# Chunked attention, low-rank mixer and channel MLP on one core: loads planned with their time on the DMA engines, and the first pair's x and low-rank part summed in PSUM

## The chip, the core and the metric

The kernel runs on one core of a Trainium2 chip. The metric is device time in microseconds (us); three runs of the kernel before gave a median of 1002.67. The profile is one execution on the same core, read by engine: PE (TensorE; its weight loads are PEld), DVE (VectorE), ACT (ScalarE), POOL (GpSimd) and SP (SyncE). SP and POOL matter here because they issue the transfers from HBM, each on a queue of its own.

## The reference

Eight batches, eight heads, 576 positions of 64 values. Attention stays within chunks of 64 positions. Its output, put together as x of 576 x 512 per batch, goes through a mixer of rank 32 over the positions, and then through an MLP over the channels (512 to 2048 and back):

```python
q_c, k_c, v_c = (a.reshape(B, H, S // 64, 64, D) for a in (q, k, v))
scores = np.matmul(q_c, k_c.transpose(0, 1, 2, 4, 3)) / np.sqrt(D)
scores = scores - np.max(scores, axis=-1, keepdims=True)
attn = np.exp(scores)
attn = attn / (np.sum(attn, axis=-1, keepdims=True) + 1e-09)
x = np.matmul(attn, v_c)                       # -> (8, 576, 512)
...
h = x.transpose(0, 2, 1) @ U @ V               # U 576x32, V 32x576
u = x + h.transpose(0, 2, 1)
out = u + np.maximum(u @ w_ch1, 0.0) @ w_ch2   # 512 -> 2048 -> 512
```

U, V and both channel weights are float64; q, k and v are float32.

## The kernel before

**Tiling.** Batches are taken in four pairs. A pair has 2 x 576 = 1152 rows, nine tiles of 128 rows (T0 to T8; tile 4 holds rows of both batches, so it has two *segments*, the others one). Three tiles form a group of 384 rows (g = 0, 1, 2). The hidden dimension is cut into 16 blocks f of 128; W0 to W15 are the pieces of both weights that belong to a block.

**A tile's way through attention.** SP loads q and k (L388, L389), POOL loads v in pair 0 (L399). PE transposes q and k (L419, written `ps_qT`, `ps_kT`), ACT copies them out, PE multiplies for the scores (`sc`, L441), DVE takes the maximum and subtracts it (L455, L459), ACT takes the exponential (L463), PE transposes that (`ps_eT`), and multiplies by v (`av`, L472); DVE divides by the sum and gives x (L490).

**Mixer.** PE forms y = transposed U times x, in plain f32 in pair 0 (L559, five products of 512 columns per batch), and ACT and DVE round it to `ys` (L574, L575). Then, for each tile, four steps: `low_rank` (L592) multiplies V by ys into a PSUM bank `u`, one product of 512 columns for each segment; `add` (L598) adds it to x on DVE; `transposed` (L604) transposes the sum on PE in four blocks of 128 x 128 into a bank `ut`; and ACT and DVE split that into a high part `uth` (L612) and a low part `utl` (L617).

**MLP.** For a group and a block f, `hidden` multiplies 12 times into a bank h (L638, 384 columns), ACT and DVE turn this into `hh` and `hl` (L646, L651), and `project_out` adds three products of 512 columns for each tile into its bank `o` (L664), which collects all 16 blocks. At the end `finish` (L676) adds x and SP stores the result. Since `add` wrote into x, this x is u.

**Weights.** The float64 words are made into f32 on the chip: one ACT pass, six DVE steps (L92 to L101) and then a rounded high part and a low part (ACT L348, DVE L351) for each piece. DVE does this beside all that is told above.

**What sets the order.** In pairs 1 to 3 the attention and mixer steps are strewn by rule between the products of the MLP. Pair 0, with all weight pieces, is ordered by a planner when the program is built. Each piece of work is an `Op` with an engine, an estimated time `us`, what it comes after, a delay `lat` before other engines may use it, and the buffers it takes and frees. `order()` gives, for one engine after another, the ready op that can start first or stands first by rank; ranks come from three lists: `LOADS` (transfers), `WORK` (T tile, P the y of a batch, M the mixing of a group, U, V, W) and `STRETCHES` (group, first and last block f of the MLP). The result is a fixed sequence on each engine, and each engine keeps it: a waiting instruction holds all behind it. Into PE's planned idle time before the first mixing the planner puts products of no use (`fill`, L138, bfloat16), 41 in all.

SP and POOL may have eight transfers each on the way; each new one waits for the one eight before it, and for its buffer.

Of the kernel before, what the change touches and what calls it, by code (L numbers as in the profile page):

```python
# [21 lines left out]
def kernel(  # L22
# [11 lines left out]
    nc = tc.nc  # L34
# [5 lines left out]
    P = 128  # L40
    C = 64
# [69 lines left out]
    rank = [0]  # L111

    class Op:
        def __init__(self, eng, us, run, *after, take="", free="", lat=0.1):
            self.eng, self.us, self.run, self.lat = eng, us, run, lat
            self.after = [o for o in after if o is not None]
            self.take, self.free = take.split(), free.split()
            self.rank = rank[0], len(ops)
            ops.append(self)
# [25 lines left out]
    def order():  # L145
        free_at = {}
        stock = {k: [0.0] * n for k, n in ROOM.items()}
        waits = {o: len(o.after) for o in ops}
        users = {o: [] for o in ops}
        for o in ops:  # L150
            for p in o.after:
                users[p].append(o)
        ready = {o: 0.0 for o in ops if not o.after}
        hot = None
        out = []
        while ready:
            best = {}
            for o, t in ready.items():
                t = max(t, free_at.get(o.eng, 0.0))
                need = {k: o.take.count(k) for k in o.take}  # L160
                if any(len(stock[k]) < n for k, n in need.items()):
                    continue
                for k, n in need.items():
                    t = max(t, sorted(stock[k])[n - 1])
                best.setdefault(o.eng, []).append((t, o))
            if not best:
                raise RuntimeError(f"the plan has no way on: {[(o.name, o.eng, o.rank, o.take) for o in ready]} {stock}")
            picks = []
            for c in best.values():
                t0 = min(t for t, _ in c) + 0.05  # L170
                picks.append(min(((t, o) for t, o in c if t <= t0), key=lambda z: z[1].rank))
            t, o = min(picks, key=lambda z: (z[0], z[1].rank))
            us = o.us
            if o.eng == "PE":
                if o.name == "hidden" and hot is None:
                    hot = t + 3.5
                us *= COLD if hot is None or t < hot else 1.0
            end = t + us
            del ready[o]
            free_at[o.eng] = end  # L180
            for k in o.take:
                stock[k].remove(min(stock[k]))
            for k in o.free:
                stock[k].append(end)
            o.start, o.end = t, end
            for u in users[o]:
                waits[u] -= 1
                if not waits[u]:
                    ready[u] = max(p.end + (p.lat if p.eng != u.eng or p.lat > 1 else 0.0) for p in u.after)
            out.append(o)  # L190
        assert len(out) == len(ops), "some of the plan is left"
        return out
# [34 lines left out]
    def u_ops():  # L227
        st = {}

        def load():  # L230
            words = wslot((10, 2 * R), U32, "uraw")
            nc.vector.memset(words[:, 4:6], 0)
            nc.gpsimd.dma_start(words[:, 0:4], moe_U[0 : 4 * P].rearrange("(t p) r -> p t r", p=P))
            nc.gpsimd.dma_start(words[0:C, 4], moe_U[4 * P : S])
            nc.gpsimd.dma_start(words[C:P, 5], moe_U[0:C])
            nc.gpsimd.dma_start(words[:, 6:10], moe_U[C:S].rearrange("(t p) r -> p t r", p=P))
            st["raw"] = words.rearrange("p t (r w) -> p t r w", w=2)

        def room():
            st["u"] = wslot((10, R), U32, "uroom")  # L240
            return st["u"]

        def whole():

            st["f"] = u32 = wslot((10, 4, R), F32, "ust32")
            v = st["u"].bitcast(F32)
            nc.gpsimd.memset(u32[:, :, 3, :], 0.0)
            for j in range(3):
                nc.scalar.copy(u32[:, :, j, :], v)
            ust32.append(u32)  # L250

        def high():
            for j in range(4):
                nc.scalar.copy(ust[:, :, j, :], st["u"].bitcast(F32))

        def low():
            nc.vector.tensor_sub(ust[:, :, 3, :], st["u"].bitcast(F32), ust[:, :, 3, :])

        ld = Op("POOL", 2.7, load, take="w", lat=2.0)
        o, _ = rounding(Later(lambda: st["raw"]), room, ld, "w", 10 * R)  # L260
        w = Op("ACT", 1.4, whole, o, take="w", free="w")
        h = Op("ACT", 1.8, high, w)
        lo = Op("DVE", 0.5, low, h, free="w")
        h.rank = lo.rank = 0.5, len(ops)
        return w
# [5 lines left out]
    def v_ops():  # L271
        nc.vector.memset(vst[:, 0:C].bitcast(F32), 0.0)
        nc.vector.memset(vst[:, C + S :].bitcast(F32), 0.0)
        n = S // 4
        st = {}

        def load():
            words = wslot((2 * n,), U32, "vraw")
            nc.gpsimd.dma_start(words, moe_V.rearrange("r (b c) -> (r b) c", b=4))
            st["raw"] = words.rearrange("p (r w) -> p r w", w=2)  # L280

        def room():
            st["v"] = wslot((n,), U32, "vroom")
            return st["v"]

        def join():
            st["rows"] = dram.tile([R, S], F32, name="vrows")
            nc.gpsimd.dma_start(st["rows"].rearrange("r (b c) -> (r b) c", b=4), st["v"].bitcast(F32))

        def spread():  # L290
            st["all"] = wslot((S,), F32, "vall")
            for j in range(4):
                nc.gpsimd.dma_start(st["all"][j * R : (j + 1) * R], st["rows"])

        def high():
            nc.scalar.copy(vst[:, C : C + S], st["all"])

        def low():
            rows = slice(2 * R, 3 * R)
            dst = vst[rows, C : C + S]  # L300
            nc.vector.tensor_sub(dst, st["all"][rows], dst)

        ld = Op("POOL", 0.7, load, take="w", lat=2.5)
        o, _ = rounding(Later(lambda: st["raw"]), room, ld, "w", n)
        o = Op("POOL", 0.6, join, o, free="w w", lat=2.5)
        o = Op("POOL", 2.0, spread, o, take="w", lat=2.5)
        o = Op("ACT", 0.7, high, o)
        return [Op("DVE", 0.77, low, o, free="w")]

# [10 lines left out]
    def w_ops(f, after=None):  # L320
        st = {}
# [9 lines left out]

        n = 1 if f < NF - XROOM else 2
        size = 2 * DM // n
        ld = Op("SP", 3.2, load, after, take="w", lat=2.0)
        halves = []
        for z in range(n):
            cols = slice(z * size, (z + 1) * size)
# [73 lines left out]
    def attention_ops(pr, t, after=None):  # L411
# [75 lines left out]
        def scaled(e):  # L487
# [9 lines left out]

        src = lambda z: loaded[pr, t][z].rearrange("p h d -> p (h d)")
        flat = lambda: st["ex"].rearrange("p a b k -> p (a b k)")
        lq = Op("SP", 3.4, lambda: load_qk(pr, t), after, take="w" if mine else "slot slot slot", lat=1.6)  # L500
        tq = Op("PE", 0.55, lambda: transpose(src(0), "qT_"), lq, begun.get((pr, t - 2)), take="bank")
        lv = Op(
            "POOL" if mine else "SP",
            2.5,
            lambda: load_v(pr, t, q_last.get(ahead.get(t)) if mine else None),
            lq,
            lat=2.2,
        )
        if mine:
            tqs[t], lvs[t] = tq, lv  # L510
# [71 lines left out]
    def mix_ops(pr, t, x, ys, after=None, first=None):  # L582
# [31 lines left out]
        def low():  # L614
            uh, ul = ut_of[pr, g]
            js = slice(j * P, (j + 1) * P)
            nc.vector.tensor_sub(ul[:, :, js], st["t"].rearrange("p (c t) -> p c t", c=NCC), uh[:, :, js])  # L617

        segs = len(list(segments(pr, t)))
        lr = Op("PE", 0.23 * segs, low_rank, x, after, *(ys[b - 2 * pr] for _, _, b, _ in segments(pr, t)), *v_done, take="bank")  # L620
        ad = Op("DVE", 0.69, add, lr, free="bank")
# [34 lines left out]
    def project_out(pr, g, f, hs, first, final, j):  # L656
        hh, hl = hs
        t = g * GT + j
        if first:
            acc[g, j] = bank(f"o_{pr}_{t}")  # L660
        js = slice(j * P, (j + 1) * P)
        prods = [(hh, 0), (hh, 1), (hl, 0)]
        for i, (h, z) in enumerate(prods):
            nc.tensor.matmul(  # L664
                acc[g, j],
                lhsT=h[:, js],
                rhs=w2[f][:, z],
                start=(first and i == 0),
                stop=(final and i == 2),
            )  # L670
        return acc[g, j]
# [42 lines left out]

    LOADS = "W0 T1 T0 T3 T4 W1 T2 V T5 T8 U W2 T6 T7 W3 W4 W5 W6 W7 W8 W9 W10 W11 W12 W13 W14 W15".split()
    WORK = "U T3 T4 T8 T5 T2 T1 T7 T0 T6 W0 P0 P1 V M0 M1 W1 W2 W3 W4 W5 W6 W7 W8 W9 W10 W11 W12 W13 W14 W15".split()
    STRETCHES = ((0, 0, 2), (1, 0, 2), (0, 2, 3), (1, 2, 3), (0, 3, 4), (1, 3, 4), (0, 4, 5), (1, 4, 5), (0, 5, 6), (1, 5, 6), (0, 6, 7), (1, 6, 7), (0, 7, 8), (1, 7, 8), (0, 8, 9), (1, 8, 9), (0, 9, 10), (1, 9, 10), (0, 10, 11), (1, 10, 11), (0, 11, 12), (1, 11, 12), (0, 12, 13), (1, 12, 13), (0, 13, 14), (1, 13, 14), (0, 14, 16), (1, 14, 16))
    GATES = (28, 30)  # L720
    BASE = 1000
    u_done = None
# [170 lines left out]
```

## Time and profile before

| | us |
|---|---|
| median of three runs (lowest, highest) | 1002.67 (1002.03, 1004.46) |
| the profiled execution | 1002.66 |
| its span | 1000.9 |
| PE busy in the span | 980.2 (98%) |
| DVE busy | 405.6 (41%) |
| ACT busy | 256.9 (26%) |
| PE's products h and o, their three largest groups together | 1048.1 with overlap |

The groups of the page give busy time and mean duration of one instruction. PE's products overlap, so that a group's sum exceeds the time that it takes on the clock, and the distance from one start to the next is the better price. The mean granted TensorE clock of the execution was 0.994. A row of the timeline gives start, duration, engine, line and operation with its count, and in brackets the idle time ahead of it and what ended it.

### The profile page before, as it was taken

The numbers are of one execution on the slowest core, as the hardware profiler recorded it, in microseconds if no ns is written. First come the engines' busy times: TensorE is split into PE (matmuls) and PEld (weight loads), VectorE is DVE, ScalarE is ACT, GpSimd is POOL, SyncE is SP. The second block draws the span as 40 slices with busy tenths as digits, with TensorE's granted clock in tenths as the row PEclk, the third lists the DMA queues.
The fourth block names the chain that finished last, engine by engine and source line by source line (L and its number), as shares of the span: only waits on it lengthen the run. The fifth ranks groups of instructions, "written<-read, shape, count | busy, mean of one in ns | idle before, by whom it ended". The sixth has DMA issues, their size and how long they took to land.

```text
span 1000.9 us, 16704 instructions
## 1 busy us (share of the span) xinstructions
PE 980.2 (98%) x7073; PEld 854.2 (85%) x7073; DVE 405.6 (41%) x813; ACT 256.9 (26%) x460; POOL 33.3 (3%) x89
## 2 busy tenths in 40 slices
PE   7799999999999999999999999999999999999998
PEld 4569999888888889888888898888888889989997
DVE  5789999652332434222333332322423233211211
ACT  4533433322322222221222221221322221111110
POOL 6500000000000000000000000000000000000000
PEclk8999999999999999999999999999999999999999
DMA  9962223152312102121120111021021000000000
GB/s 223 225 207 73 97 84 115 23 148 54 64 33 64 32 5 60 32 46 52 35 62 35 30 32 32 35 62 33 32 65 32 32 1 1 32 1 1 32 1 32
DMA packets 121914, 56.42 MB, mean 56 GB/s; under 512 B 106208, under 2 KB 114432, under 8 KB 121840
## 3 DMA queue, kind: packets, MB, share of 16 engines
q1 hardware_dynamic: 120320, 52.18, 20.5%
q0 software_dynamic: 1520, 3.17, 1.5%
q8 instruction: 56, 0.92, 0.4%
q14 instruction: 18, 0.15, 0.0%
HBM read 45.83 MB, written 9.51 MB: 55 GB/s over the span
## 4 chain that ended last, share of the span: by engine, by line
PE 71%; DVE 0%; ACT 0%; DVEq 0%; issue 0%; ACTq 0%
PE h L638 31%; PE o L664 31%; PE av L472 1%; PE sc L441 1%; PE ut L604 1%; PE ps_eT L419 1%; PE ps_qT L419 1%; PE ps_kT L419 1%; PE u L592 1%; PE y L552 1%; PE y L553 1%; DVE x L676 0%; DVE ex L459 0%; ACT ex L463 0%; DVEq L888 0%; DVE mx L455 0%
## 5 line engine op out<-in xcount | busy, mean ns | idle before, releaser
L638 PE MATMUL h<-uth,w 128*128 128x384 f32 x1536 | 425.2, 341 | 0.4 <-DVE x L490 0.3
L664 PE MATMUL o<-w,hh 128*128 128x512 f32 x1152 | 363.5, 403 | 0.0
L638 PEld LDWEIGHTS h<-uth,w 128*128 128x128 f32 x1536 | 281.3, 188 | 8.5 <-issue 0.8
L651 DVE SCALAR_TENSOR_TENSOR hl<-h,hh 128x384 fp32r<-128x384 f32 x192 | 106.7, 556 | 429.9 <-ACT hh L646 429.8
L638 PE MATMUL h<-utl,w 128*128 128x384 f32 x768 | 259.4, 338 | 0.0
L664 PEld LDWEIGHTS o<-w,hh 128*128 128x128 f32 x1152 | 207.7, 188 | 34.9
L646 ACT ACTIVATE hh<-h 128x384 fp32r<-128x384 f32 x192 | 94.3, 491 | 481.9 <-PE h L638 481.8
L664 PE MATMUL o<-w,hl 128*128 128x512 f32 x576 | 217.7, 395 | 0.0
L638 PEld LDWEIGHTS h<-utl,w 128*128 128x128 f32 x768 | 144.4, 188 | 6.3 <-DVE utl L617 0.3
L664 PEld LDWEIGHTS o<-w,hl 128*128 128x128 f32 x576 | 108.3, 188 | 24.8
L463 ACT ACTIVATE ex<-ex 128x512 f32<-128x512 f32 x36 | 22.7, 632 | 87.4 <-DVE ex L459 87.3
L455 DVE TENSOR_REDUCE mx<-sc 128x4 f32<-128x256 f32 x72 | 27.9, 417 | 31.7 <-PE sc L441 31.7
L598 DVE TENSOR_TENSOR x<-u,x 128x512 f32<-128x512 f32 x36 | 24.3, 684 | 27.1 <-PE u L592 26.8
L617 DVE TENSOR_TENSOR utl<-ut,uth 128x512 fp32r<-128x512 f32 x36 | 24.4, 688 | 20.3 <-ACT uth L612 20.3
L433 ACT COPY eT<-ps_eT 128x512 f32<-128x512 f32 x36 | 21.0, 587 | 37.4 <-PE ps_eT L419 37.2
L545 DVE TENSOR_TENSOR xl<-x,xh 128x512 fp32r<-128x512 f32 x30 | 20.5, 688 | 23.6 <-ACT xh L541 20.5
L612 ACT CAST uth<-ut 128x512 fp32r<-128x512 f32 x36 | 20.8, 588 | 31.6 <-PE ut L604 31.6
L459 DVE TENSOR_TENSOR ex<-sc,mx 128x256 f32<-128x256 f32 x72 | 27.9, 417 | 1.2 <-DVE mx L455 0.5
L490 DVE TENSOR_TENSOR x<-av,sm 128x256 f32<-128x256 f32 x72 | 27.2, 418 | 1.1
L386 POOL MEMSET vn<- 128x8 f32 x27 | 3.0, 113 | 698.9 <-PE y L553 171.1
L676 DVE TENSOR_TENSOR x<-o,x 128x512 f32<-128x512 f32 x36 | 23.3, 684 | 5.8 <-PE o L664 5.8
L348 ACT CAST w<-wroom 128x1024 fp32r<-128x1024 f32 (+1 forms) x19 | 17.1, 915 | 27.4 <-DVE wroom L101 27.4
(88 smaller groups left out, 606.6 us busy)
## 6 DMA issues: line engine op xcount, KB each, us to landing
wraw<-in_moe_w_ch_dram SPq DMA_DIRECT2D x32, 512.0 KB, 4.7
out_dram<-x SPq DMA_DIRECT2D x36, 256.0 KB, 2.1
vn<-in_v_dram SPq DMA_DIRECT2D x108, 64.0 KB, 2.8
qn<-in_q_dram SPq DMA_DIRECT2D x24, 256.0 KB, 3.4
kn<-in_k_dram SPq DMA_DIRECT2D x24, 256.0 KB, 4.0
qkv<-in_v_dram POOLq DMA_DIRECT2D x36, 64.0 KB, 6.6
qkv<-in_q_dram SPq DMA_DIRECT2D x8, 256.0 KB, 8.9
qkv<-in_k_dram SPq DMA_DIRECT2D x8, 256.0 KB, 8.0
```

What stands on the lines that cost most here:

```text
L419: o = nc.tensor.transpose(ps[:, j * P : (j + 1) * P], src[:, j * P : (j + 1) * P], ident)
L455: nc.vector.reduce_max(mx, st["sc"][e], axis=AX.X)
L459: nc.vector.tensor_sub(st["ex"][:, :, e, :], st["sc"][e], mx.unsqueeze(2).broadcast_to([P, HP, C]))
L463: nc.scalar.activation(exf, exf, AF.Exp, scale=SCALE)
L490: nc.vector.tensor_mul(st["x"][:, :, e, :], st["av"][e][:, :, 0:D], st["sm"][:, e].unsqueeze(2).broadcast_to([P, HP, D]),)
L598: nc.vector.tensor_add(x, st["u"], x)
L617: nc.vector.tensor_sub(ul[:, :, js], st["t"].rearrange("p (c t) -> p c t", c=NCC), uh[:, :, js])
L638: nc.tensor.matmul(ps[:, :GN], lhsT=w[:, z, cc], rhs=u[:, cc, :], start=(n == 0), stop=(n == 3 * NCC - 1))
L646: nc.scalar.activation(hh, ps[:, :GN], AF.Relu)
L651: nc.vector.scalar_tensor_tensor(hl, ps[:, :GN], 0.0, hh, op0=ALU.max, op1=ALU.subtract)
L664: nc.tensor.matmul(acc[g, j], lhsT=h[:, js], rhs=w2[f][:, z], start=(first and i == 0), stop=(final and i == 2),)
L676: nc.vector.tensor_add(x, ps, x)
```

## The change

Two things are changed, both in pair 0 alone.

**The planner's transfers.** An `Op` may now have a time `dma`. The planner adds these up one after another (`moved`), and what depends on a load is ready when the load has been issued and its share of that one stream has passed. A load's time on its engine gets shorter in turn: q and k of a tile from 3.4 us to 1.25, with 2.36 of DMA, a weight piece from 3.2 to 1.25 with 3.1, v with 1.18. The three lists are new. The MLP starts with three blocks of each group in place of two. These figures are the planner's; they change nothing but the order.

**The mixing.** `joined` takes the place of `low_rank`, `add` and `transposed`. For each block of 128 columns PE multiplies the block of x by the identity, as an ordinary f32 product and not as a transpose, and then adds V times ys into the same PSUM block, already transposed: with ys as the stationary operand and 128 columns of V moving. x is no longer changed, so the low-rank part must reach the output in another way: `project_out` starts each bank `o` of pair 0 with one product of V and ys for each segment (512 columns), ahead of the first MLP product. The pairs 1 to 3 still use the old steps. In the built program 36 transposed blocks, 10 low-rank products and 9 additions go; 36 products with the identity, 40 low-rank products of 128 columns and 10 of 512 columns come; and `fill` is there 47 times.

```diff
+            self.dma = dma
...
+            if o.dma:
+                moved = max(moved, t) + o.dma
+            o.there = max(end, moved) if o.dma else end
...
-                    ready[u] = max(p.end + (p.lat if p.eng != u.eng or p.lat > 1 else 0.0) for p in u.after)
+                    ready[u] = max(p.there + (p.lat if p.eng != u.eng or p.lat > 1 else 0.0) for p in u.after)
...
-        ld = Op("SP", 3.2, load, after, take="w", lat=2.0)
+        ld = Op("SP", 1.25, load, after, take="w", lat=1.8, dma=3.1)
...
-        lq = Op("SP", 3.4, lambda: load_qk(pr, t), after, take="w" if mine else "slot slot slot", lat=1.6)
+        lq = Op("SP", 2.5 if t == 4 else 1.25, lambda: load_qk(pr, t), after, take="w" if mine else "slot slot slot", lat=1.8, dma=2.36)
...
+        def joined():
+            x = x_of[pr, t]
+            st["t"] = pt = bank("ut_" + n)
+            segs = list(segments(pr, t))
+            for cc in range(NCC):
+                cs = slice(cc * P, (cc + 1) * P)
+                nc.tensor.matmul(pt[:, cs], lhsT=x[:, cs], rhs=ident, start=True, stop=False)
+                for i, (r, m, b, s0) in enumerate(segs):
+                    a = C + s0 - r
+                    nc.tensor.matmul(
+                        pt[:, cs],
+                        lhsT=y_of[pr, b - 2 * pr][:, cs],
+                        rhs=vst[:, a : a + P],
+                        start=False,
+                        stop=(i == len(segs) - 1),
+                    )
+
+        if pr == 0:
+            tr = Op(
+                "PE", 1.1 + 0.44 * len(list(segments(pr, t))), joined, x, after, *(ys[b - 2 * pr] for _, _, b, _ in segments(pr, t)), *v_done, take="bank"
+            )
+            hi = Op("ACT", 0.59, high, tr, after, take="" if j else "ut")
+            lo = Op("DVE", 0.69, low, hi, free="bank")
...
+            return [[tr], [tr, hi, lo]]
...
             acc[g, j] = bank(f"o_{pr}_{t}")
+            if pr == 0:
+                for i, (r, m, b, s0) in enumerate(segments(pr, t)):
+                    a = C + s0 - r
+                    nc.tensor.matmul(
+                        acc[g, j], lhsT=vst[:, a : a + P], rhs=y_of[pr, b - 2 * pr], start=(i == 0), stop=False
+                    )
...
-                start=(first and i == 0),
+                start=(first and i == 0 and pr > 0),
...
-    LOADS = "W0 T1 T0 T3 T4 W1 T2 V T5 T8 U W2 T6 T7 W3 W4 W5 W6 W7 W8 W9 W10 W11 W12 W13 W14 W15".split()
+    LOADS = "T1 T0 U W0 T3 T2 T5 W1 T4 T7 W2 T6 W3 W4 W5 T8 W6 W7 V W8 W9 W10 W11 W12 W13 W14 W15".split()
```

Three places of the new order. The first is SP's queue at the end of pair 0's tiles, from the third weight piece on (`wraw` are the words of a piece, `qkv_7` is the buffer of tile 7). Before:

```order
L325 DMA wraw_562<-in_moe_w_ch_dram 128x4x256
L329 DMA wraw_562<-in_moe_w_ch_dram 128x1024
L388 DMA qkv_6_622<-in_q_dram 128x8x64
L389 DMA qkv_6_622<-in_k_dram 128x8x64
L388 DMA qkv_7_682<-in_q_dram 128x8x64
L389 DMA qkv_7_682<-in_k_dram 128x8x64
L325 DMA wraw_767<-in_moe_w_ch_dram 128x4x256
```

And now:

```order
L330 DMA wraw_241<-in_moe_w_ch_dram 128x4x256
L334 DMA wraw_241<-in_moe_w_ch_dram 128x1024
L393 DMA qkv_6_273<-in_q_dram 128x8x64
L394 DMA qkv_6_273<-in_k_dram 128x8x64
L393 DMA qkv_8_333<-in_q_dram 128x8x64
L394 DMA qkv_8_333<-in_k_dram 128x8x64
L330 DMA wraw_582<-in_moe_w_ch_dram 128x4x256
```

Tile 8 has changed places with tile 7 as the last; nine tiles and three weight pieces stand ahead of the fourth piece in both.

The second place is PE from the last tile's q to the first product o (`y_0` and `y_1` are the two batches' y, `u` a low-rank product, `h_0_0` and `h_0_1` the blocks 0 and 1 of group 0; the rows left out are of the same kinds). Before:

```order
L419 MATMUL ps_qT_7_805<-ident,qkv_7_682 128x128 x4
L419 MATMUL ps_kT_7_811<-ident,qkv_7_682 128x128 x4
L559 MATMUL y_0_480<-x_4_557,ust_146 128x512
L559 MATMUL y_1_566<-x_5_737,ust_146 128x512
...
L592 MATMUL u_0_854<-ys_0_825,vst 128x512
...
L604 MATMUL ut_0_925<-ident,x_0_468 128x128 x4
...
L559 MATMUL y_1_566<-x_7_942,ust_146 128x512
...
L638 MATMUL h_0_0_961<-uth_0_939,w_244 128x384
...
L638 MATMUL h_0_1_997<-uth_0_939,w_863 128x384
...
L604 MATMUL ut_5_1021<-ident,x_5_737 128x128 x4
L664 MATMUL o_0_1027<-w_244,hh_0_0_984 128x512 x2
```

And now, where between `ps_kT_8` and the first `ut_0` stand the transposed exponentials of tiles 7, 6 and 8, the products av of the tiles 2, 5, 4, 7, 6 and 8, the scores of tile 8, five products y and four fills:

```order
L424 MATMUL ps_qT_8_684<-ident,qkv_8_333 128x128 x4
L424 MATMUL ps_kT_8_694<-ident,qkv_8_333 128x128 x4
...
L477 MATMUL av_0_8_892<-qkv_8_333,eT_8_851 64x65 x2
...
L631 MATMUL ut_0_919<-ident,x_0_489 128x128
L634 MATMUL ut_0_919<-vst,ys_0_880 128x128
...
L565 MATMUL y_1_884<-x_6_910,ust_340 128x512
...
L670 MATMUL h_0_0_983<-uth_0_941,w_551 128x384
...
L696 MATMUL o_0_1035<-ys_0_880,vst 128x512
L702 MATMUL o_0_1035<-w_551,hh_0_0_1016 128x512 x2
L702 MATMUL o_0_1035<-w_551,hl_0_0_1019 128x512
```

The low-rank products no longer stand ahead of the transposition but inside it, block by block; six products av, where there were two, stand behind the last tile's q; and only one h instead of two stands ahead of the first o.

The third place is DVE ahead of `hl_0_0`, the low part that the first o products need last (`wroom` and `wraw` are the words of a weight piece in conversion, the low part of a finished piece is `w`). Before:

```order
L575 TENSOR_TENSOR ys_1_957<-y_1_566,ys_1_957 32x512
L598 TENSOR_TENSOR x_3_440<-u_3_885,x_3_440 128x512
L351 TENSOR_TENSOR w_863<-wroom_510,w_863 128x1024
L92 TENSOR_SCALAR wroom_675<-wroom_675 128x1024
L93 TENSOR_SCALAR wroom_675<-wroom_675 128x1024
L651 SCALAR_TENSOR_TENSOR hl_0_0_995<-h_0_0_961,hh_0_0_984 128x384
```

And now:

```order
L581 TENSOR_TENSOR ys_1_979<-y_1_884,ys_1_979 32x512
L96 SCALAR_TENSOR_TENSOR wroom_692<-wraw_241,wroom_692 128x1024
L99 TENSOR_SCALAR wraw_241<-wroom_692 128x1024
L100 SCALAR_TENSOR_TENSOR wraw_241<-wraw_241 128x1024
L101 TENSOR_TENSOR wroom_692<-wroom_692,wraw_241 128x1024
L683 SCALAR_TENSOR_TENSOR hl_0_0_1019<-h_0_0_983,hh_0_0_1016 128x384
```

Four steps of the third piece's conversion have moved ahead of it, and the addition is gone.

More of the change, by code (lines that the diff above doesn't have):

```diff
@@ L113, with __init__ @@
     class Op:
-        def __init__(self, eng, us, run, *after, take="", free="", lat=0.1):
+        def __init__(self, eng, us, run, *after, take="", free="", lat=0.1, dma=0.0):
             self.eng, self.us, self.run, self.lat = eng, us, run, lat
+            self.dma = dma
             self.after = [o for o in after if o is not None]
@@ L154, in order @@
         hot = None
+        moved = 0.0
         out = []
@@ L257, in low @@
             nc.vector.tensor_sub(ust[:, :, 3, :], st["u"].bitcast(F32), ust[:, :, 3, :])
-        ld = Op("POOL", 2.7, load, take="w", lat=2.0)
+        ld = Op("POOL", 2.5, load, take="w", lat=1.8, dma=1.0)
         o, _ = rounding(Later(lambda: st["raw"]), room, ld, "w", 10 * R)
@@ L301, in low @@
             nc.vector.tensor_sub(dst, st["all"][rows], dst)
-        ld = Op("POOL", 0.7, load, take="w", lat=2.5)
+        ld = Op("POOL", 0.6, load, take="w", lat=1.8, dma=0.5)
         o, _ = rounding(Later(lambda: st["raw"]), room, ld, "w", n)
-        o = Op("POOL", 0.6, join, o, free="w w", lat=2.5)
-        o = Op("POOL", 2.0, spread, o, take="w", lat=2.5)
+        o = Op("POOL", 0.6, join, o, free="w w", lat=2.2, dma=0.2)
+        o = Op("POOL", 2.0, spread, o, take="w", lat=1.8, dma=1.0)
         o = Op("ACT", 0.7, high, o)
@@ L506, in attention_ops @@
             lq,
-            lat=2.2,
+            lat=1.8,
+            dma=1.18,
         )
@@ L617, in low @@
             nc.vector.tensor_sub(ul[:, :, js], st["t"].rearrange("p (c t) -> p c t", c=NCC), uh[:, :, js])
+        def joined():
[20 more added lines that the diff above has]
+            lo = Op("DVE", 0.69, low, hi, free="bank")
+            if t == 0:
+                Op("PE", 0.01, end_filling, tr, free="bank")
+            return [[tr], [tr, hi, lo]]
         segs = len(list(segments(pr, t)))
@@ L711 @@
     Op.name = ""
-    LOADS = "W0 T1 T0 T3 T4 W1 T2 V T5 T8 U W2 T6 T7 W3 W4 W5 W6 W7 W8 W9 W10 W11 W12 W13 W14 W15".split()
-    WORK = "U T3 T4 T8 T5 T2 T1 T7 T0 T6 W0 P0 P1 V M0 M1 W1 W2 W3 W4 W5 W6 W7 W8 W9 W10 W11 W12 W13 W14 W15".split()
-    STRETCHES = ((0, 0, 2), (1, 0, 2), (0, 2, 3), (1, 2, 3), (0, 3, 4), (1, 3, 4), (0, 4, 5), (1, 4, 5), (0, 5, 6), (1, 5, 6), (0, 6, 7), (1, 6, 7), (0, 7, 8), (1, 7, 8), (0, 8, 9), (1, 8, 9), (0, 9, 10), (1, 9, 10), (0, 10, 11), (1, 10, 11), (0, 11, 12), (1, 11, 12), (0, 12, 13), (1, 12, 13), (0, 13, 14), (1, 13, 14), (0, 14, 16), (1, 14, 16))
+    LOADS = "T1 T0 U W0 T3 T2 T5 W1 T4 T7 W2 T6 W3 W4 W5 T8 W6 W7 V W8 W9 W10 W11 W12 W13 W14 W15".split()
+    WORK = "T0 V T2 U T8 T3 T1 T5 T4 W0 T7 P0 M0 T6 W1 W2 W3 P1 M1 W4 W5 W6 W7 W8 W9 W10 W11 W12 W13 W14 W15".split()
+    STRETCHES = ((0, 0, 3), (1, 0, 3), (0, 3, 4), (1, 3, 4), (0, 4, 5), (1, 4, 5), (0, 5, 6), (1, 5, 6), (0, 6, 7), (1, 6, 7), (0, 7, 8), (1, 7, 8), (0, 8, 9), (1, 8, 9), (0, 9, 10), (1, 9, 10), (0, 10, 11), (1, 10, 11), (0, 11, 12), (1, 11, 12), (0, 12, 16), (1, 12, 16))
     GATES = (28, 30)
```

## The prediction

> **What bounds the kernel now.** I read the page first: its busy times, its chain that ended last and its costliest groups.
>
> ```profile
> PE 980.2 (98%) x7073; PEld 854.2 (85%) x7073; DVE 405.6 (41%) x813; ACT 256.9 (26%) x460; POOL 33.3 (3%) x89
> PE 71%; DVE 0%; ACT 0%; DVEq 0%; issue 0%; ACTq 0%
> L638 PE MATMUL h<-uth,w 128*128 128x384 f32 x1536 | 425.2, 341 | 0.4 <-DVE x L490 0.3
> L664 PE MATMUL o<-w,hh 128*128 128x512 f32 x1152 | 363.5, 403 | 0.0
> ```
>
> TensorE is the bound over the whole span, and the channel products h and o fill it without gaps. An instruction added to PE therefore costs its time, and one removed gives it back, except where PE waits anyway. Where that is, the stretches tell (columns: PE, PEld, DVE, ACT, POOL busy, granted clock, DMA share, GB/s).
>
> ```profile
> 0.00:50.00 50.00, 38.26 (x557) 24.94 (x557) 32.39 (x86) 25.74 (x46) 28.60 (x60) 0.93 1.12 224
> 45.00:50.00 5.00, 1.17 (x11) 0.82 (x8) 1.39 (x3) 2.13 (x4) 3.21 (x6) 1.00 1.17 231
> 50.00:55.00 5.00, 4.93 (x66) 2.84 (x67) 1.96 (x7) 0.00 (x0) 1.67 (x3) 0.66 1.07 274
> 70.00:75.00 5.00, 4.33 (x26) 3.74 (x27) 4.97 (x8) 1.77 (x4) 0.00 (x0) 1.00 0.46 172
> 75.00:175.00 100.00, 100.00 (x502) 90.41 (x501) 95.09 (x122) 37.56 (x52) 0.00 (x0) 1.00 0.28 92
> 190.00:195.00 5.00, 4.32 (x53) 3.43 (x52) 0.74 (x2) 1.55 (x3) 0.00 (x0) 1.00 0.46 105
> 195.00:200.00 5.00, 4.16 (x22) 3.34 (x22) 2.13 (x6) 1.60 (x3) 0.00 (x0) 1.00 0.00 0
> 205.00:210.00 5.00, 4.73 (x57) 4.21 (x56) 2.77 (x8) 1.56 (x3) 0.11 (x1) 1.00 0.61 152
> ```
>
> Until 50 us PE is busy 38.3 of 50 us, part of it with fills, while the DMA engines are full (share 1.12) at 224 GB/s: this stretch belongs to the DMA. From 75 to 175 us PE is solid. Around 190 to 210 us it idles 0.68 + 0.84 + 0.27 = 1.8 us. The waits between 0 and 76 us agree: the longest group is for v, and the one that the change removes by construction (the transposition behind DVE's addition) is 0.6 us.
>
> ```profile
> PE av L472 <- DMA qkv<-in_v_dram: 4.4, 3, 2.0
> PE ut L604 <- DVE x L598: 0.6, 1, 0.6
> ```
>
> So the question is: when does PE become solid in the new order, and how much work is behind it then? What comes last on SP's queue of pair 0's tiles are q and k of tile 7 (the fourth row: the time to landing of the one k issued between 42 and 46 us; the fifth, from the page, is what POOL's queue moves in all, in MB).
>
> ```profile
> 36.66 3.72 SPq L388 DMA_DIRECT2D qkv<-in_q_dram  x1
> 40.44 2.17 SPq L389 DMA_DIRECT2D qkv<-in_k_dram  x1
> 42.71 3.15 SPq L325 DMA_DIRECT2D wraw<-in_moe_w_ch_dram  x1
> qkv<-in_k_dram SPq DMA_DIRECT2D x1, 256.0 KB, 8.7
> q0 software_dynamic: 1520, 3.17, 1.5%
> ```
>
> k of tile 7 is issued at 42.6 and lands at 51.3 us. In the timeline of PE its transposition comes only at 55.13, behind other waits.
>
> ```profile
> 50.07 1.17 PE L472 MATMUL av<-qkv,eT 64*64 64x65 f32 x30 [1.85 <-DMA qkv<-in_v_dram]
> 55.13 0.60 PE L419 MATMUL ps_qT<-ident,qkv 128*128 128x128 f32 x4
> 56.00 1.88 PE L559 MATMUL y<-x,ust 128*128 128x512 f32 x4
> 57.82 0.69 PE L441 MATMUL sc<-qkT 64*64 64x64 f32 x32
> 58.44 0.65 PE L419 MATMUL ps_eT<-ident,ex 128*128 128x128 f32 x4
> 58.85 0.94 PE L592 MATMUL u<-ys,vst 128*128 128x512 f32 x3
> 63.85 0.70 PE L472 MATMUL av<-qkv,eT 64*64 64x65 f32 x32
> 64.48 1.53 PE L604 MATMUL ut<-ident,x 128*128 128x128 f32 x12
> 65.89 1.99 PE L559 MATMUL y<-x,ust 128*128 128x512 f32 x4
> 70.45 0.94 PE L592 MATMUL u<-ys,vst 128*128 128x512 f32 x3
> 71.22 0.34 PE L638 MATMUL h<-uth,w 128*128 128x384 f32 x1
> 74.10 1.25 PE L604 MATMUL ut<-ident,x 128*128 128x128 f32 x8 [0.60 <-DVE x L598]
> 75.11 0.71 PE L664 MATMUL o<-w,hh 128*128 128x512 f32 x2
> 75.65 0.40 PE L664 MATMUL o<-w,hl 128*128 128x512 f32 x1
> 75.89 0.39 PE L664 MATMUL o<-w,hh 128*128 128x512 f32 x1
> ```
>
> Prices on PE are distances between starts here: q and k transposed 0.87 us (55.13 to 56.00), a y product in plain f32 0.91 (56.00 to 57.82 for two), scores of a tile 0.62, eT 0.41, av 0.63, a transposed 128x128 0.1175 (64.48 to 65.89 for twelve), a low-rank product u 0.26 (70.45 to 71.22 for three), an o product of 512 columns 0.24, an h of 384 columns 2.2 to 2.3 (71.22 to 74.10 less the wait of 0.60). The first o starts at 75.11, and by then both h of the first group are done.
>
> **The change part by part.** *Removed*, on PE: 10 low-rank products (0.26 each, 2.6 us) and 36 transposed blocks (4.2 us), 6.8 us together. On DVE: nine additions, and the one wait of 0.6 us on them. DVE's time is no gain by itself: PE was solid beside it from 75 us on.
>
> Two more groups, of the first 100 us, are needed for what is added: the weight loads of y, and the fills.
>
> ```profile
> L559 PEld LDWEIGHTS y<-x,ust 128*128 128x128 f32 x20 | 3.4, 201 | 2.5 <-issue 2.1
> L138 PE MATMUL ps_fill<-fill 128*128 128x512 bf16 x41 | 13.2, 473 | 1.3 <-DVE fill L131 1.3
> ```
>
> *Added*: 36 products of a block of x with the identity, in plain f32 and not as transposes. No row shows that with 128 columns. By columns it is a quarter of a y product, 0.23 us, and I take that, since both are plain f32 with a 128x128 stationary block. Below it cannot be under a transposed block, 0.1175. From above, if the two weight loads that a y product issues (20 for ten products, 201 ns each) set the pace, it is 0.40.
>
> 40 products of vst with ys, 128 columns: a quarter of an o product is 0.06, a single load at those 201 ns 0.20; I take 0.1175, the nearest row in shape. A one-segment tile then costs 4 x (0.23 + 0.1175) = 1.4 us, tile 4 with two segments 1.9; pair 0 in all 13.0 (6.6 to 22). Ten seeds of 512 columns: 2.4 us. PE's work so grows by 13.0 + 2.4 - 6.8 = 8.6 us (from 2 to 18).
>
> The Trainium skill speaks against this form: "Perfetto Trace Analysis", section Transposes, says to use the transpose for a transposition and not a standard matmul, since it skips the arithmetic. The trace agrees by half: 0.1175 against 0.23 a block; at the transpose's price the sum would be 4.1 us lower. Its page "TensorE: Matmul & The Clock Gate", section Back-to-back issue gap, gives about 81 ns for a product of 128 columns with its load; with it the 40 products would cost 1.5 us less than by the row.
>
> *Moved*: the loads. SP now ends with tile 8 instead of tile 7; the bytes ahead are the same (nine tiles and three pieces, 7.9 MB), beside 3.2 MB on POOL's queue. In the new order SP waits less for buffers (3.72 us at q of tile 7 before), but the engines were full anyway. At 224 GB/s all 11.0 MB are there at 49.2 us; at the earliest with POOL 0.55 MB behind, 46.7; at the latest, with W3 sharing as before, 51.3. I take 49.2.
>
> PE takes its orders in sequence, so q8 and k8 hold what stands behind them in the order: q8 and k8 (0.87), eT7, eT6, eT8 (1.2), six av (3.8), sc8 (0.6), five y (4.55), four fills (0.32 each by their row, 1.3): 12.4 us to the first joined tile. Then joined 0 to 2 (4.2), three y (2.7), joined 3 (1.4), h (2.2), joined 4 and 5 (3.3): 13.8. First o at 49.2 + 26.2 = 75.4, as late as before, but behind it still lie one h that was done before (2.2), ten seeds (2.4) and the joined tiles 6 to 8 over what they replace, 3 x (1.4 - 0.26 - 0.47) = 2.0. That is +0.3 + 6.6 = +6.9 us. The late idle of 1.8 us hangs on ACT and DVE; the nine additions are done long before, while the changed stretches of f may shift it: I take half, 0.9, between none and all. T1 ahead of W0 on SP, and the 43 other fills where 41 were, cost nothing: the DMA stretch up to L covers them. Were that cover gone, the two fills would be 0.6 us.
>
> Sum: +6.0 us on the profiled execution's 1002.66 (span 1000.9), which is the median of the runs, 1002.67, within 0.01: 1008.7. In general the change is L - 43.2, with L the landing of tile 8's k. A measurement here tells about 0.3%, 3.0 us (999.7 to 1005.7).
>
> **The rivals.** *Tile 8 lands early (faster).* POOL's v loads fall back behind SP's, whose issue no longer stops for buffers, and L comes to 39: 39 - 43.2 gives -4.2, 998.5. It decides at L under 40.2. For it: the removed stops. Against it: 7.9 MB by 40 us leaves POOL 1.1 MB of its 3.2 at the rate of the first 50 us, and v8, POOL's last, must still be there when av8's turn comes at L + 11.8.
>
> *Nothing measurable.* L about 43, or joined blocks near the price of a transposed block (6.4 us less) with L at 49: 1002.5. For it: the first row of the stretches, 11.7 us not busy until 50, which a better plan could use for work that now stands behind q8. Against it: the order puts 12.4 us there.
>
> *The joined blocks are bound by their weight loads:* at 0.40 and 0.20 pair 0 costs 9 us more, 1017.5. For it: a block of 128 columns streams for less time than its load takes. Against it: twelve transposed blocks, each with a load of its own, stand 0.1175 apart.
>
> *DVE becomes late.* In its new order the rest of the conversion of W2 stands ahead of the low part of h(0,0), which the third o product needs:
>
> ```profile
> 74.56 1.21 DVE L96 SCALAR_TENSOR_TENSOR wroom<-wraw,wroom 128x1024 uint32<-128x1024 uint32 x1
> 77.36 0.68 DVE L99 TENSOR_SCALAR wraw<-wroom 128x1024 uint32<-128x1024 uint32 x1
> 78.07 1.23 DVE L100 SCALAR_TENSOR_TENSOR wraw<-wraw 128x1024 f32<-128x1024 uint32 x1
> 79.33 1.22 DVE L101 TENSOR_TENSOR wroom<-wroom,wraw 128x1024 f32<-128x1024 f32 x1
> ```
>
> These 4.3 us stand behind ys of the second batch, whose y products end at L + 19.3. With 1.8 us for that ys and the low part itself (an estimate, from subtractions as long as the 0.68 above) the low part is there at L + 25.4, and the third o product starts at L + 26.2 + 0.24 (a seed) + 0.48. So there is one us to spare: a slip of 3 us would cost 2, 1010.7.
>
> **How the numbers follow.** Forecast (L 46.7 to 51.3 at my prices, 1006 to 1011) 0.48; early landing 0.20; nothing measurable 0.20; weight-bound blocks 0.05; late DVE 0.07. Faster 0.20, same 0.20, slower 0.60. The likeliest is 1008.7. The range 999.5 to 1015 leaves out most of the early landing and the upper end of the weight-bound case.
>
> **What would show it.** In the profile after: k of tile 8 landing at 47 to 51 us, with its transposition waiting for that DMA; L631 at about 0.23 between starts of its kind beside L634 at 0.12; the first joined tile at 60 to 63 and the first o at 74 to 78 us, with no longer stop between; PE's instructions 8 to 9 us more in pair 0; some idle gone at 190 to 210. I am wrong if PE has passed q8 by 42 us, if a joined tile takes under 0.8 us or over 2, or if PE stops for DVE between the first joined tile and 90 us.

## The result: slower by 1.0%

The changed kernel takes 1012.09 us (median of four runs, 1011.6 to 1014.83), the one before 1003.09 on the same chip. The ratio is 1.0103 with a 95% interval of 1.0084 to 1.0121, and so some 8 to 12 us were lost where 6.0 were forecast. The two profiled executions have spans of 1009.8 and 1000.9 us: 8.9 us apart. Each later comparison is a ratio to the kernel before on the same chip, since the medians of that kernel itself moved between 1002.7 and 1003.6.

First the page after, the lines that answer to those of before, and one of its DMA queues.

```profile
PE 987.4 (98%) x7145; PEld 863.4 (86%) x7155; DVE 401.3 (40%) x804; ACT 256.6 (25%) x460; POOL 33.7 (3%) x89
L670 PE MATMUL h<-uth,w 128*128 128x384 f32 x1536 | 424.6, 340 | 0.0
L702 PE MATMUL o<-w,hh 128*128 128x512 f32 x1152 | 363.3, 403 | 0.0
q8 instruction: 56, 0.92, 0.4%
```

TensorE is still the bound, and its channel products cost what they did: nothing happened to them but that they start later. PE's busy time grew by 7.2 us, and DVE's fell by 4.3. The stretches show where the start went (columns as before: PE, PEld, DVE, ACT, POOL busy, granted clock, DMA share, GB/s).

```profile
45.00:50.00 5.00, 3.80 (x42) 2.57 (x42) 1.31 (x5) 3.23 (x5) 2.46 (x4) 0.66 1.19 248
50.00:55.00 5.00, 2.83 (x98) 2.52 (x100) 2.44 (x10) 1.68 (x4) 0.00 (x0) 1.00 0.90 251
55.00:60.00 5.00, 4.99 (x74) 2.52 (x73) 3.37 (x11) 0.63 (x1) 0.00 (x0) 0.66 0.79 232
190.00:195.00 5.00, 5.00 (x25) 4.38 (x25) 1.43 (x3) 0.62 (x2) 0.11 (x1) 1.00 0.00 0
195.00:200.00 5.00, 5.00 (x44) 4.79 (x42) 1.94 (x3) 2.02 (x4) 0.00 (x0) 1.00 0.00 0
```

From 50 to 55 us, where I had PE solid, it is busy for 2.83 us, and from 55 to 60 it runs at two thirds of the clock. The idle time around 195 us is gone. PE's timeline gives the same row by row, from the last tile's q to the first product for o:

```profile
48.53 0.87 PE L424 MATMUL ps_qT<-ident,qkv 128*128 128x128 f32 x4
50.27 0.63 PE L424 MATMUL ps_kT<-ident,qkv 128*128 128x128 f32 x4 [0.87 <-DMA qkv<-in_k_dram]
52.68 0.68 PE L446 MATMUL sc<-qkT 64*64 64x64 f32 x26 [0.25 <-DVE sm L490]
55.01 0.34 PE L446 MATMUL sc<-qkT 64*64 64x64 f32 x6 [1.66 <-issue]
55.87 3.64 PE L565 MATMUL y<-x,ust 128*128 128x512 f32 x4
59.45 0.70 PE L477 MATMUL av<-qkv,eT 64*64 64x65 f32 x32
65.78 0.38 PE L631 MATMUL ut<-ident,x 128*128 128x128 f32 x2
66.61 0.33 PE L634 MATMUL ut<-vst,ys 128*128 128x128 f32 x1 [0.45 <-DVE vst L306]
67.11 0.44 PE L631 MATMUL ut<-ident,x 128*128 128x128 f32 x2
67.31 0.31 PE L634 MATMUL ut<-vst,ys 128*128 128x128 f32 x1
67.45 0.44 PE L631 MATMUL ut<-ident,x 128*128 128x128 f32 x2
79.61 0.44 PE L696 MATMUL o<-ys,vst 128*128 128x512 f32 x1
```

k of tile 8 landed at 50.15 us, inside the range given, and PE waited for it as forecast, though for 0.87 us only: its q was there when PE came to it at 48.53, so that an earlier k alone could have brought no more than that. In the midst of tile 8's scores PE then stopped for 1.66 us, for nothing that the profile names. The two y products behind it took 3.58 us in place of 1.82. In the first joined tile PE waited 0.45 us for DVE, which had made V (`vst`) late: V's loads stand far back in the new lists. The first product for o starts at 79.61; before it was 75.11.

### The profile page after: what moved, and what is told of

It is laid out like the page before. It is cut to its first block, busy times and chain, and to the rows that moved or that the text cites. A ratio compares the mean times of both kernels' runs of the same rounds, so it can differ in the third digit from the quotient of the medians.

```text
span 1009.8 us, 16850 instructions
## 1 busy us (share of the span) xinstructions
PE 987.4 (98%) x7145; PEld 863.4 (86%) x7155; DVE 401.3 (40%) x804; ACT 256.6 (25%) x460; POOL 33.7 (3%) x89
## 4 chain that ended last, share of the span: by engine, by line
PE 71%; DVE 0%; ACT 0%; DVEq 0%; issue 0%; ACTq 0%
PE h L670 31%; PE o L702 31%; PE av L477 1%; PE sc L446 1%; PE ut L610 1%; PE ps_eT L424 1%; PE ps_qT L424 1%; PE ps_kT L424 1%; PE u L598 1%; PE y L558 1%; PE y L559 1%; DVE x L714 0%; DVE ex L464 0%; ACT ex L468 0%; DVEq L926 0%; DVE mx L460 0%
## 5 line engine op out<-in xcount | busy, mean ns | idle before, releaser
L702 PEld LDWEIGHTS o<-w,hl 128*128 128x128 f32 x576 | 108.1, 188 | 25.4 <-DVE hl L683 0.7
L604 DVE TENSOR_TENSOR x<-u,x 128x512 f32<-128x512 f32 x27 | 18.5, 685 | 26.6 <-PE u L598 26.4
L404 POOL DMA_DIRECT2D qkv<-in_v_dram x36 | 23.1, 649 | 10.6 <-DMA qkv<-in_v_dram 2.8
```

What stands on the lines that cost most here:

```text
L404: d = queue.dma_start(vn[e * C : (e + 1) * C, c, :, 0:D], v[b, e::2, s0 : s0 + C, :].rearrange("h s d -> s h d"),)
L702: nc.tensor.matmul(acc[g, j], lhsT=h[:, js], rhs=w2[f][:, z], start=(first and i == 0 and pr > 0), stop=(final and i == 2),)
```

## The experiments

They come in three questions: which part of the change costs the time; what the joined form costs, and where a cheaper one goes; what the stop at 53 us is.

**The mixing of before under the new plan.** `joined` and the seeds are taken out of the changed kernel.

```diff
-        if pr == 0:
+        if False:
             tr = Op(
                 "PE", 1.1 + 0.44 * len(list(segments(pr, t))), joined, x, after, ...
...
-            if pr == 0:
+            if False:
                 for i, (r, m, b, s0) in enumerate(segments(pr, t)):
...
-                start=(first and i == 0 and pr > 0),
+                start=(first and i == 0),
```

> The changed planner and its three lists, with the mixing of the kernel before (low-rank product, addition, transposition; no seeds). Theory ORDER (mine): the new order of loads and products itself is late, since 12 us of products stand behind the last tile's q and k: 1005 to 1011 us, the first h at 68 to 72 us, with new waits of PE for DVE's additions between av8 and the first h. Theory WORK: the order is neutral, and only the work that the joined form adds to PE (about 8 us by rows) was paid: 1001 to 1003.5 us, the first h within 1 us of the 67.3 of before.

Measured: 1016.26 us, ratio 1.0126 (1.0101 to 1.0151). With 8 us less work on PE it is no faster than the whole change (the two intervals overlap), and it is beyond either expectation. The waits of PE between 85 and 215 us, and one stretch of it:

```profile
PE ut L610 <- DVE x L604: 2.3, 1, 2.3
PE u L598 <- DVE x L604: 0.8, 1, 0.8
85.00:100.00 15.00, 10.64 (x43) 8.24 (x43) 14.60 (x18) 4.34 (x6) 0.00 (x0) 0.78 0.21 71
```

DVE is full (14.60 of 15 us) with the conversion of weights, the additions wait in its queue, and PE waits for them: 4.4 us idle in 15, with the clock down to 0.78. So theory WORK is refuted: with the old mixing the new order is late by itself. But much of the loss here lies in waits for additions, which the changed kernel does not have in pair 0. This run prices the order with the old mixing, and not the order's share in the change.

**The joined form under the old plan.** `joined` and the seeds, as in the diff of the change, are put into the kernel before; planner and lists stay.

> The planner's rules and lists of before, with the joined form and its seeds. Theory ORDER: part of the 8 us of added work falls into the waits that PE had between 58 and 75 us (about 2.5 us): 1006 to 1009.5 us. Theory WORK: all of it is paid: 1010 to 1013 us. In both a one-segment tile takes 1.3 to 1.4 us, and a seed 0.23.

Measured: 1007.02 us, ratio 1.0036 (1.0022 to 1.0049), as theory ORDER had it: a tile takes 1.34 us and a seed 0.23, and 4 of the 8 us are not paid. The wait of 0.6 us for the addition is gone, the idle time around 195 us too, and the rest falls where PE had waited between 58 and 65 us.

**The new rules alone, and the new rules with the joined form.** Both keep the three lists of before (`LOADS`, `WORK`, `STRETCHES`) and take the changed planner; the first has the old mixing, the second the joined form.

```diff
-    LOADS = "T1 T0 U W0 T3 T2 T5 W1 T4 T7 W2 T6 ...".split()
+    LOADS = "W0 T1 T0 T3 T4 W1 T2 V T5 T8 U W2 ...".split()
```

> The new rules for the time of loads with the lists and the mixing of before. If the parts add up (joined form 3.6, joined form with the new rules 9.2), this is 5 to 6.5 us over the kernel before, 1008 to 1009.5. If the old mixing suffers more under the new order, as it did with the new lists (12.6), 10 us or more over it. If the rules only hurt together with the joined form, within 3 us of it.

> The changed kernel with the three lists of before: the joined form and the new rules for the time of loads. If the lists carry the loss of the order, this is like the joined form alone, 1006 to 1008 us. If the rules do (they let the last q and k land at 36 us in the plan), 1010 to 1013 us, with PE again waiting for q or k ahead of work that is ready.

Measured: the rules alone 1006.26 us, 1.0033 (1.0017 to 1.0049); the rules with the joined form 1011.94, 1.0092 (1.0079 to 1.0105). The first lies between my first and third reading: less than the sum would have it, but more than nothing. The second cannot be told from the whole change, so with the joined form the new lists neither help nor hurt; with the old mixing they do hurt, 1.0126 against 1.0033. With 3.6 us for the joined form alone and 3.3 for the rules, 2 us are left for the two together, which is no more than the uncertainty of the three ratios. Both kernels have a stop as in the changed kernel, after 30 of the 32 score products of a tile; the first two rows are of the rules with the joined form, the third of the rules alone:

```profile
51.90 0.64 PE L446 MATMUL sc<-qkT 64*64 64x64 f32 x30
53.74 0.33 PE L446 MATMUL sc<-qkT 64*64 64x64 f32 x2 [1.20 <-issue]
53.37 0.33 PE L446 MATMUL sc<-qkT 64*64 64x64 f32 x2 [1.45 <-issue]
```

**The plan told of later landings.** Each tile's q and k in the changed kernel land 1.3 us later in the plan than the tile's before it.

```diff
-        lq = Op("SP", 2.5 if t == 4 else 1.25, ..., lat=1.8, dma=2.36)
+        lq = Op("SP", 2.5 if t == 4 else 1.25, ..., lat=1.8 + 1.3 * [1, 0, 3, 2, 5, 4, 7, 6, 8].index(t), dma=2.36)
```

> The changed kernel, where the planner is told that each further tile of pair 0 lands 1.3 us later than the one before it (10.4 us for the last). The work is the same; of the products between the last tile's q and the first joined tile four instead of thirteen groups are left there, and a fill or two less. Theory ORDER: PE has done more before the last tile lands, the first o product starts 5 us or more earlier, and the kernel takes 1004 to 1009 us. Theory WORK, or a bound by DVE's conversions behind: 1010.5 to 1013 us.

Measured: 1008.62 us, ratio 1.0045 (1.003 to 1.006), within theory ORDER. Four rows of PE: q and k of tile 8, the first joined tile and the first seed.

```profile
55.21 0.60 PE L424 MATMUL ps_qT<-ident,qkv 128*128 128x128 f32 x4
55.64 0.60 PE L424 MATMUL ps_kT<-ident,qkv 128*128 128x128 f32 x4
60.37 0.38 PE L631 MATMUL ut<-ident,x 128*128 128x128 f32 x2
73.03 0.79 PE L696 MATMUL o<-ys,vst 128*128 128x512 f32 x1
```

No load is waited for here any more, and between k and the first joined tile lie 4.7 us, where the changed kernel had 15.5. The first seed is 6.6 us earlier; two joined tiles now stand behind it (3.1 us), and 3.5 us come out at the end by the medians and 3.6 by the profiled spans (5.8 by the two ratios). This kernel also has neither the stop at 53 us nor the half clock behind it, which together are 3.3 us in the changed kernel. So the gain need not come from having less work behind the last tile: the run with more fills, below, keeps the order of the changed kernel, loses the stop and the half clock, and comes to 1008.86 us. That the order of work around the last tile decides is not shown.

**x by a transpose.** In `joined` the block of x enters PSUM by a transpose; the low-rank product still adds to it.

```diff
-                nc.tensor.matmul(pt[:, cs], lhsT=x[:, cs], rhs=ident, start=True, stop=False)
+                nc.tensor.matmul(pt[:, cs], lhsT=x[:, cs], rhs=ident, is_transpose=True, start=True, stop=False)
```

> The changed kernel with the block of x brought into PSUM by a transpose in place of the f32 product with the identity; the low-rank product still adds to it. If the price of a block is that of its columns and passes (0.20 as a product, 0.12 or less as a transpose), a one-segment tile falls from 1.34 to about 1.03 us and the kernel by 2.5 to 3.0 us, to 1009 to 1009.6. If the joined blocks are bound by weight loads, the tile stays above 1.25 and the time within 1 us of 1012.1.

```profile
67.40 0.30 PE L631 MATMUL ut<-ident,x 128*128 128x128 f32 x1
67.46 0.31 PE L634 MATMUL ut<-vst,ys 128*128 128x128 f32 x1
67.60 0.30 PE L631 MATMUL ut<-ident,x 128*128 128x128 f32 x1
PE o L702 <- DVE hl L683: 1.8, 2, 1.5
PE h L670 <- DVE utl L623: 0.2, 1, 0.2
```

A block with its low-rank part takes 0.20 us in place of 0.335, a tile 0.80 in place of 1.34: more than either expectation, 4.9 us for nine tiles. The kernel takes 1010.86 us, ratio 1.0063 (1.0045 to 1.0081); between the two ratios lie 4 us, between the two medians 1.2, so that some 1 to 4 of the 4.9 us came through; part of that may be the stop in tile 8's scores, 0.42 us here in place of 1.66. A part of what is missing shows in the waits (the last two rows, 0 to 90 us): PE now waits 2.0 us for low parts from DVE.

The rule of "Perfetto Trace Analysis", section Transposes, in the Trainium skill (use a transpose, not a standard matmul) is borne out by these rows: 0.135 us a block.

**The same under the two better plans.** The edit is the same, in the two kernels with the joined form under the old plan and with the later landings.

> Planner and lists of before, the joined form with x brought in by a transpose. A one-segment tile takes 0.80 us by the run with the transposed x, in place of 1.34: 4.9 us less work on PE. Theory PE: PE is the bound behind the last tile, and 4 to 4.9 us come back from 1007.0: 1002 to 1003 us. Theory DVE: as in the changed kernel with the transposed x, where 1.2 us of the same 4.9 came back and PE then waited for the low parts from DVE: 1005.5 to 1007 us with waits of o or h for DVE of 1.5 us or more.

> The plan with later landings, and x brought in by a transpose. Theory PE: 4 to 4.9 us less than 1008.6: 1003.7 to 1004.6. Theory DVE: DVE is at 4.9 of each 5 us from 60 us on and gets no less to do, so PE waits for it behind the joined tiles: 1006.5 to 1008.6 us.

Measured: 1006.4 us, 1.0041 (1.0028 to 1.0055), and 1008.39, 1.0056 (1.0036 to 1.0077): neither differs from its untransposed kernel. Waits of PE in the first, 0 to 90 us:

```profile
PE y L559 <- DVE x L490: 1.6, 2, 1.3
PE o L696 <- DVE hl L677: 1.3, 2, 0.9
```

Without the transpose the same two waits are 0.7 and 0.4 us, so they take 1.8 of the 4.9 us: PE comes sooner to values that DVE has not made yet, as theory DVE has it, but where the rest went is not shown. For the plan with later landings theory DVE is not borne out: its profiled execution, the fastest of four (1005.34 us), waits 0.2 us for a low part up to 90 us. Its four times spread over 5.6 us, and what took the 4.9 us there stays open.

**Only the end of STRETCHES.** The kernel before, with the changed kernel's last entries.

```diff
-... (0, 12, 13), (1, 12, 13), (0, 13, 14), (1, 13, 14), (0, 14, 16), (1, 14, 16))
+... (0, 12, 16), (1, 12, 16))
```

> The kernel before; only the last entries of its STRETCHES are those of the changed kernel (blocks 12 to 15 of a group in one stretch). If the idle time of PE at 190 to 210 us (1.8 us) went by this list alone, it is under 0.4 us here and the kernel is 1 to 1.8 us under the one before. If it went because DVE had no additions left to do, it stays at 1.5 us or more, and the time is unchanged.

Measured: 1006.56 us, 1.0034 (1.0021 to 1.0047): slower, which neither reading had. Its profiled execution was the fastest of eight (1002.93 us), so its rows do not explain the median. They do show that the idle time did not simply go: PE is idle for 3.2 us between 180 and 190 us (2.72 and 4.11 of 5 us busy), and waits 1.7 us there for a weight piece. That fits the new list, in which a group's last four blocks follow one another.

```profile
PE h L638 <- ACT w L348: 1.7, 1, 1.7
```

In the joined form under the old plan, with the old list, PE had no idle time from 185 to 210 us, and in the one with the new rules as well it had 1.6 us. What removed the 1.8 us in the changed kernel is neither this list nor the missing additions by themselves; it stays open.

**Later q and k in the old plan.**

```diff
-        lq = Op("SP", 3.4, ..., lat=1.6)
+        lq = Op("SP", 3.4, ..., lat=3.0)
```

> The kernel before, where its planner takes 3.0 us in place of 1.6 from a load of q and k to its use. Theory ORDER: what the kernel before loses between 44 and 65 us are products that wait for late loads while others are ready, and a later planned landing is nearer to the truth: 999 to 1002 us. If its order is already as good as the loads allow, 1002 to 1005 us.

Measured: 1005.11 us, ratio 1.0018 (1.0007 to 1.0029). The order before is not helped by it; no kernel here is faster than the one before.

**32 more fills.** The last question is the stop at 53 us. In the changed kernel it stands after 26 of the 32 score products of tile 8, in the kernel with the old mixing under the new plan and in the one with x by a transpose after the same 26. In each of them, and in the two kernels with the new rules and the old lists, a record of 16,384 bytes of the instruction queue (`q8` in the page) had ended 1.3 to 1.5 us before PE went on: at 53.5 and 55.01, 55.1 and 56.62, 56.0 and 57.29, 52.3 and 53.74, 51.9 and 53.37 us. The page's 56 such records are 0.92 MB; PE has 14,300 matmuls and weight loads, which makes 255 for a record. So I moved PE's stream.

```diff
-            fill(int(0.7 * (o.start - idle) / FILL))
+            fill(int(0.7 * (o.start - idle) / FILL) + getattr(o, "more", 0))
...
         tq = Op("PE", 0.55, lambda: transpose(src(0), "qT_"), lq, begun.get((pr, t - 2)), take="bank")
+        if (pr, t) in ((0, 3), (0, 6)):
+            tq.more = 24 if t == 3 else 8
```

> The changed kernel with 32 more fills on PE, 24 ahead of q of tile 3 and 8 ahead of q of tile 6, where PE waits for a load anyway. They put 64 more instructions into PE's stream ahead of tile 8. Theory FETCH: PE's stop after 26 of the 32 score products of tile 8 is a wait for its own instructions, which come in pieces by DMA; it then stands 64 instructions earlier in the program, among the products av of tile 5 (or nowhere), and no longer in the scores of tile 8. Theory OTHER (a buffer, ACT or DVE): it stays after the 26th product. With the clock granted in full from 13 us to the first joined tile, the half-clock stretch of 3.2 us at 56 us goes as well: 1009 to 1012 us by the first, 1011 to 1013 by the second.

```profile
50.15 0.65 PE L424 MATMUL ps_qT<-ident,qkv 128*128 128x128 f32 x4
50.64 0.60 PE L424 MATMUL ps_kT<-ident,qkv 128*128 128x128 f32 x4
53.02 0.69 PE L446 MATMUL sc<-qkT 64*64 64x64 f32 x32 [0.25 <-DVE sm L490]
53.53 0.85 PE L477 MATMUL av<-qkv,eT 64*64 64x65 f32 x32
54.32 1.98 PE L567 MATMUL y<-x,ust 128*128 128x512 f32 x4
62.57 0.39 PE L633 MATMUL ut<-ident,x 128*128 128x128 f32 x2
76.39 0.44 PE L698 MATMUL o<-ys,vst 128*128 128x512 f32 x1
45.00:50.00 5.00, 4.49 (x72) 2.82 (x65) 4.02 (x11) 1.70 (x4) 3.65 (x7) 1.00 1.12 239
55.00:60.00 5.00, 4.95 (x79) 2.95 (x79) 3.72 (x15) 2.65 (x5) 0.11 (x1) 1.00 1.03 350
```

The 32 scores of tile 8 run through. The record that had come at 52.0 to 53.5 now comes at 47.2 to 48.6. The clock is full from 45 to 60 us (last two rows), and the two y products take 1.91 us in place of 3.58. Stop and half clock together are 1.66 + 1.67 = 3.3 us; the first product for o is 3.2 us earlier, and the kernel takes 1008.86 us, a hair under the first reading, ratio 1.0060 (1.0045 to 1.0076). A full clock is bound up with the fills: the run does not part the two shares.

In this run the stop is gone rather than moved, and the fills shift the times of the other engines too, so by itself it does not name the cause. The place of the stop does. These rows count PE's work from the start into the stop, in the changed kernel and in the new rules alone (the first two figures in brackets: matmuls, some of whose records are missing, and weight loads):

```profile
0.00:54.50 54.50, 38.39 (x582) 26.17 (x591) 31.96 (x83) 26.95 (x48) 30.65 (x62) 0.91 1.10 229
0.00:53.00 53.00, 39.89 (x588) 26.53 (x592) 33.12 (x86) 27.04 (x48) 30.55 (x62) 0.90 1.13 231
```

All five kernels that stop do so after 591 or 592 weight loads, though they follow two different orders of work. The other eight, the kernel before among them, come to that place 1.9 us or more after their last such record had ended (3.9 us in the run with more fills), and none of them stops there. A buffer, ACT or DVE would not hold PE at one count of its own instructions, so theory FETCH stands: PE waits there for its next instructions. Not all idle time that the profile calls issue is explained by this: the kernel with the old mixing under the new plan has 1.66 us of it at 34.6 us, at another place in the program.

## Why the prediction was right, and where its sizes were off

*The sign, and the step that gives it.* PE in order, held by tile 8's q and k, with 26.2 us of products from there to the first o. In the kernel with more fills, which has neither stop nor half clock, it is 76.39 - 50.15 = 26.2 us, where 50.15 is the start of q's row (by chance the same figure as the landing in the changed kernel; PE waits for no load there). That the sum held this closely is in part luck. It had no term for the 0.45 us in which PE waits for `vst`, and it took five y at 4.55 us (4.8 there); the fills (0.32 us each taken, ten in 2.15 us there) and the joined tiles were priced too high by about as much.

*The price of the joined form.* Taken: 1.4 us a tile, 1.9 with two segments, 0.24 a seed. Measured: 1.34, 1.74 and 0.23. The block of x was 0.20 (0.23 taken), the low-rank one 0.14 (0.1175 taken). The work added to PE is 8.0 us at these prices, 8.6 at mine.

*L.* Taken 49.2, measured 50.15. One row I read wrongly: the time to landing counts from the start of the issue's row, so that k of tile 7 in the kernel before landed at 49.1 and not 51.3 us. The estimate by volume did not use it, but its upper bound did. The forecast takes every microsecond of L as one of the whole. PE came to q of tile 8 only at 48.53, after 2.4 us of waiting for the q of the tile before, so a k that alone landed earlier would have brought 0.87 us at most.

*The step that failed by size is "first o at L + 26.2".* In the changed kernel it was 29.5 us after k landed. What I had left out is the stop (1.66 us) and the clock behind it, which was at half from 55.8 to 59.2 us; I had read 0.66 in the stretch 50 to 55 of before, and had made no term of it.

*The late idle time.* I took half of 1.8 us as gone; all of it went.

The account of the 8.9 us between the spans: first product for o 4.5 later, one h 2.1, ten seeds 2.3, joined tiles 6 to 8 over what they replace 1.9, idle time -1.8, together 9.0. Against the forecast of 6.0 the first term is 4.2 more (some 0.9 of it from L, 3.3 from stop and clock), the last 0.9 less and the rest 0.3 less. So the range held the time, while the forecast lies under the measured interval of 8.4 to 12.1 us. With the stop and the half clock away the loss is 6.0 us (1.0060), as forecast; that the later L and the larger gain in late idle time cancel is luck.

*The signs.* k of tile 8 landed where I said. The first joined tile at 65.78 and the first o at 79.61 us lie outside 60 to 63 and 74 to 78, and there was a longer stop between. I had also named a stop of PE for DVE between the first joined tile and 90 us as a sign of being wrong, and there is one: 0.45 us for `vst` at 66.61. It is not the late conversion that I had feared, but V was a term that I had put at nothing.

*The rivals.* Early landing: refuted, 50.15 us. Weight-bound blocks: refuted, 0.20 and 0.14 us. Late DVE: the low part of h(0,0) was made by 79.69 us, and the product that takes it started at 80.35: 0.66 us to spare and no wait. I had called it one us; my own figures, 25.4 and 26.9 us behind L, give 1.5. With the cheaper block of x the spare was gone, and there PE waited 1.5 us for it. In the rival "nothing measurable" my sum at L of 49 gives 1002.1 us, and not 1002.5.

## What to carry to other kernels

A load that comes last holds whatever stands behind its first use on an in-order engine, so count that work as a sum of row distances from the first use; here this sum came within 0.1 us, with errors that cancelled. Cheaper work on one engine need not come back where the next value comes from another engine: 4.9 us less on PE gave nothing measurable under two of three plans, and under one of them waits for DVE took 1.8 us of it. When a kernel with another order is faster, look in its trace for stops that it happens to miss before the order gets the credit: the plan with later landings and the one with 32 more fills cannot be told apart in time.

## What the runs showed of the hardware

PE can stop for its own instructions: five of the thirteen kernels stopped 0.4 to 1.7 us in the midst of 32 equal products, each after 591 or 592 weight loads, and went on 1.3 to 1.5 us after a 16 KB record of the instruction queue had ended. The Trainium skill, "Runtime: NRT & Kernel Launch", section Instruction fetch mechanics, says that instructions come in blocks of 16 KiB in sequence. The trace agrees (56 records of 16,384 bytes). It also says that this is hidden by the pace of issue; at these five places it was not. The DMA share between the record's end and PE's going on was 0.94 in the changed kernel and 0.40 in the one with the old mixing under the new plan, so that full DMA engines are not shown to be needed for it.

Behind the pause of PE of 1.66 us, which followed others of 2.4 and 0.9, the clock was granted at a half for 3.4 us, from 55.8 to 59.2 us, though PE was busy by then. In the two kernels with the new rules and the old lists it stayed full after pauses of 1.20 and 1.45 us; what starts a half-clock stretch is not settled by these runs. A transpose into PSUM can be followed by a product that adds to it, at 0.20 us for the two.
